# Attention scores as three rounded products of 256 columns instead of one full fp32 product of 192

## The chip, the cores and the metric

The kernel runs on one NeuronCore of a Trainium2 chip, with its engines TensorE (PE, with the weight loads shown apart as PEld), VectorE (DVE), ScalarE (ACT), GpSimd (POOL) and SyncE (SP, which here issues most of the transfers). The metric is the device time of one execution in microseconds; less is better.

## The reference

Local and global attention for 8 batches of 8 heads, followed by a two-layer network on all tokens. Only the parts that the change touches or waits for are kept:

```python
k_all = concat([k_g, k_l]);  v_all = concat([v_g, v_l])          # 32 global + 512 local keys, head_dim 64
out_g = softmax(q_g @ k_all.T / 8) @ v_all                       # 32 global queries see all keys
s_ll  = where(abs(i - j) <= 32, q_l @ k_l.T / 8, -1e9)           # local queries: a band of +-32 ...
s_lg  = q_l @ k_g.T / 8                                          # ... and all global keys
out_l = softmax(concat([s_lg, s_ll])) @ concat([v_g, v_l])
x = heads side by side of concat([out_g, out_l])                 # 4352 tokens x 512
h = x @ w_in;  g = max(h, 0) + log1p(exp(-abs(h)))               # 512 -> 2048
return g @ w_out                                                 # 2048 -> 512
```

## The kernel before

**The network part.** Tokens are handled in eight batches `b` of 512 local tokens, and a ninth of the 256 global ones. In a batch, 16 slices `f` of 128 hidden columns follow each other. `hpart` makes `h` for a slice by 12 matmuls of 512 columns, `act` turns it into `e` (three ACT passes, one DVE pass) and splits it into a high half `gh` (a cast on ACT to fp32r, the rounded 4-byte type that TensorE streams in one pass) and a low half `gl` (a subtraction on POOL). `opart` makes the output from the products `gh*wo_high`, `gh*wo_low` and `gl*wo_high`, 12 matmuls a slice, one or two slices later. The weights are split in the same way (`split_w`: casts on ACT, L498, subtractions on POOL, L499) while batch 0 runs; the last of them is `wo15`.

**The attention part.** Heads are taken in 32 pairs `m`, head 0 on partitions 0 to 63 and head 1 on 64 to 127. Pairs 0 to 5 run ahead of the network in a way of their own. Pairs 6 to 31 are cut in pieces that are dealt out between the matmuls of the network: three score pieces `(m, p)`, p = 0 to 2, then the maxima, probabilities, sums, `values` and `normalise`. A score piece takes one tile `raw` of queries and keys (544 columns for p = 0 and 1, 448 for p = 2), and makes two parts of scores, each for both heads: 128 keys stand still as weights and 192 query columns stream past them (96 in the second part of p = 2). For pairs 8 and later the mask is added on DVE (L325) on the way from the accumulator `s_ps` to `s`, then a transposing maximum goes to `mt` (L326).

**What sets the order.** PE, ACT, DVE, POOL and SP each run their instructions strictly in the order in which they were placed. A scheduler sets the order on each engine by its own estimate of when an operation could start; the PE order follows the text of the kernel. `fold` copies `mt` (or `zt`, the sums) between partition groups on POOL (L339), reduces it on DVE (L342 to L346) and spreads it (L352); then come two transposes `mb` (L360). `normalise` reads the values' accumulator `v_ps` on DVE (L407 to L409). Once the first output accumulators of the network are open, early in batch 0, `s_ps` and `v_ps` share one accumulator tile, `ps_a` tag "a", so the first score piece of the next pair waits until L409 is done.

**Tiles.** `raw` has three buffers. `pl.tile(..., tag="x", bufs=2)` names a place with two buffers; the early pairs used "x" for their exponentials. All matmuls go through the helper `mm`, so they stand under its line (L127) in the profile. One fp32 matmul is shown as two matmul instructions with two weight loads, an fp32r matmul as one of each.

Of the kernel before, what the change touches and what calls it, by code (L numbers as in the profile page):

```python
# [8 lines left out]
F32 = mybir.dt.float32  # L9
F32R = mybir.dt.float32r  # L10
# [3 lines left out]
ALU = mybir.AluOpType  # L14
# [5 lines left out]
P = 128  # L20
# [4 lines left out]
QW = (288, 288, 192)  # L25
KWID = (256, 256, 256)
# [3 lines left out]

M0 = 6
MPE = 8
VAL = 22
TOT = 18
STEP = 3
# [14 lines left out]
def windows(ap2d, start, stride, count, width):  # L50
    base = ap2d[:, start:start + width]
    return bass.AP(base.tensor, base.offset, [list(base.ap[0]), [stride, count], [1, width]])
# [3 lines left out]
def moe_over_global_local_attention(  # L56
# [11 lines left out]
    nc = tc.nc  # L68
    PSUM = bass.MemoryType.PSUM
    const = ctx.enter_context(tc.tile_pool(name="const", bufs=1))  # L70
    pl = ctx.enter_context(tc.tile_pool(name="pl", bufs=2))
# [20 lines left out]
    for o, w, base, sign in ((32, 32, 0, 1), (64, 32, -96, -1), (96, 128, 32, 1), (96, 128, 32, -1)):  # L92
        r = mask0[:, 0, 1, o:o + w]
# [26 lines left out]
    def after(i, what):  # L120

        if what in order:
            tc.add_manual_dep(i.ins, order[what].name, mybir.DependencyInfo(mybir.DependencyClass.NoSync, mybir.DependencyReason.DATA), reason="order")
        return i

    def mm(*a, **k):
        order["pe"] = after(nc.tensor.matmul(*a, **k), "pe").ins  # L127


    M = B * H // 2  # L130
    st = {}
# [153 lines left out]
    def load(m, p):  # L285
        w = QW[p] + KWID[p]
        raw = pl.tile([P, 544], F32, tag="raw", name=f"raw{m}_{p}", bufs=3)
        order["load"] = nc.sync.dma_start(out=raw[:, :w], in_=qk[m - M0, :, EW[p]:EW[p] + w]).ins
        st["raw", m, p] = raw

    def load_v(m):
        t = pl.tile([P, 2, 6, D], F32, tag="v", name=f"v{m}", bufs=2)
        nc.sync.dma_start(out=t.rearrange("p h c d -> p (h c d)"), in_=v[m - M0])
        st["v", m] = t

    def scores(m, p):
        raw = st.pop(("raw", m, p))
        q = QW[p]
        if "o" not in banks:
            ps = ps_s.tile([P, 2, 512], F32, tag=("oA", "oB")[(3 * m + p) % 2], name=f"s_ps{m}_{p}")  # L300
        else:
            ps = ps_a.tile([P, 2, 512], F32, tag="a", name=f"s_ps{m}_{p}")
        parts = ((0, 0, 192), (192, 96, 192 if p < 2 else 96))
        pe_mask = m < MPE
        masks = (mask[:, 0:192], mask[:, 192:384] if p < 2 else mask5)
        for i, (o, qs, w) in enumerate(parts):
            ks = q + 128 * i
            for h in range(2):
                r = slice(64 * h, 64 * h + 64)
                mm(ps[:, h, o:o + w], lhsT=raw[r, ks:ks + P], rhs=raw[r, qs:qs + w],  # L310
                   start=True, stop=not pe_mask, skip_group_check=True)
            for h in range(2 if pe_mask else 0):
                mm(ps[:, h, o:o + w], lhsT=ident, rhs=masks[i], start=False, stop=True, skip_group_check=True)
        if p == 0:
            st["mt", m] = pl.tile([P, 348], F32, tag="mt", name=f"mt{m}", bufs=2)
            nc.gpsimd.memset(windows(st["mt", m], 0, 36, 3, 3), LOW)
        mt = st["mt", m]
        nb = 12 if p < 2 else 9
        s = pl.tile([P, 2, 32 * nb], F32, tag="s" if p < 2 else "s2", name=f"s{m}_{p}", bufs=4 if p < 2 else 2)
        if pe_mask:  # L320
            nc.scalar.copy(s, ps[:, :, 0:32 * nb])  # L321
        else:
            for o, mk in ((0, mask[:, 0:384]),) if p < 2 else ((0, mask[:, 0:192]), (192, mask5)):
                w = mk.shape[1]
                nc.vector.tensor_tensor(s[:, :, o:o + w], ps[:, :, o:o + w], mk.unsqueeze(1).to_broadcast([P, 2, w]), op=ALU.add)  # L325
        order["scores"] = nc.vector.tensor_reduce(windows(mt, 3 + 12 * p, 36, 2, nb), s.rearrange("p h (b k) -> p h b k", k=32),  # L326
                                axis=AX.X, op=ALU.max, apply_transpose=True).ins
        st["s", m, p] = s
# [20 lines left out]
    def maxima(m):  # L349
        e = fold(st.pop(("mt", m)), ALU.max)  # L350
        for a in range(1, 4):
            i = nc.vector.tensor_copy(e[32 * a:32 * a + 32, 0:42], e[0:32, 0:42]).ins  # L352
        order["maxima"] = i
        st["e", m] = e

    def probs(m, p):
        s, e = st["s", m, p], st["e", m]
        k = QW[p] // 32
        mb = pl.tile([P, 2, 288], F32, tag="mb", name=f"mb{m}_{p}", bufs=2)
        nc.vector.transpose(mb[:, :, :QW[p]].rearrange("p h (s k) -> p h s k", k=32),  # L360
                            windows(e, 7 * p, 21, 2, k).unsqueeze(3).to_broadcast([P, 2, k, 32]))
        for h in range(2):
            if p < 2:
                sw = s[:, h].rearrange("p (c w) -> p c w", w=192)
                nc.gpsimd.tensor_tensor(sw, sw, windows(mb[:, h], 0, 96, 2, 192), op=ALU.subtract)  # L365
        if p == 2:
            nc.gpsimd.tensor_tensor(s[:, :, 0:192], s[:, :, 0:192], mb[:, :, 0:192], op=ALU.subtract)
            nc.gpsimd.tensor_tensor(s[:, :, 192:288], s[:, :, 192:288], mb[:, :, 96:192], op=ALU.subtract)
        nc.scalar.activation(s, s, AF.Exp, scale=0.125)  # L369
        if p == 0:  # L370
            st["zt", m] = pl.tile([P, 348], F32, tag="zt", name=f"zt{m}", bufs=2)
            nc.gpsimd.memset(windows(st["zt", m], 0, 36, 3, 3), 0.0)
        nb = 12 if p < 2 else 9
        nc.vector.tensor_reduce(windows(st["zt", m], 3 + 12 * p, 36, 2, nb), s.rearrange("p h (b k) -> p h b k", k=32),  # L374
                                axis=AX.X, op=ALU.add, apply_transpose=True)

    def totals(m):
        e = fold(st.pop(("zt", m)), ALU.add)
        nc.vector.tensor_scalar(e[0:32, 0:42], e[0:32, 0:42], 1e-9, None, op0=ALU.add)
        nc.vector.reciprocal(e[0:32, 0:42], e[0:32, 0:42])  # L380
        for a in (2, 3, 1):
            o = 21 * (a // 2)
            nc.vector.tensor_copy(e[32 * a:32 * a + 32, 0:21], e[0:32, o:o + 21])
        rb = st["rb", m] = pl.tile([P, 640], F32, tag="rb", name=f"rb{m}", bufs=1)
        nc.vector.transpose(rb.rearrange("p (s k) -> p s k", k=32), e[:, 0:20].unsqueeze(2).to_broadcast([P, 20, 32]))

    def values(m):

        vt = st["v", m]
        ps = st["vs", m] = ps_a.tile([P, 2, 512], F32, tag="a", name=f"v_ps{m}")  # L390
        flat = ps.rearrange("p a q -> p (a q)")
        for p in range(NPC):
            s = st.pop(("s", m, p))
            for i, (o, qs, w) in enumerate(((0, 0, 192), (192, 96, 192 if p < 2 else 96))):
                c = OUT[p] + qs
                for h in range(2):
                    mm(flat[64 * h:64 * h + 64, c:c + w], lhsT=vt[:, h, 2 * p + i], rhs=s[:, h, o:o + w],
                       start=p < 2 and i == 0, stop=True, skip_group_check=True)
# [17 lines left out]
    def pieces():  # L416
        def piece(*fs):
            def go():
                for f in fs:
                    f()  # L420
            return go
        ps = []
        for m in range(M0, M):
            for p in range(NPC):
                fs = [lambda m=m, p=p: scores(m, p)]
                if m + 1 < M:
                    fs.append(lambda m=m, p=p: load(m + 1, p))
                if p == 2:
                    fs.append(lambda m=m: maxima(m))
                    fs += [lambda m=m, q=q: probs(m, q) for q in range(NPC)]  # L430
                ps.append((12 * m + 4 * p, piece(*fs)))
            ps.append((12 * m + TOT, lambda m=m: totals(m)))
            fs = [lambda m=m: values(m), lambda m=m: normalise(m)]
            if m + 2 < M:
                fs.append(lambda m=m: load_v(m + 2))
            ps.append((12 * m + VAL, piece(*fs)))
        ps.sort(key=lambda t: t[0])
        return ps
# [173 lines left out]
    def loads(upto):  # L612
        while wk[0] < min(upto, len(order_w)):
            if order_w[wk[0]]:
                load_w(*order_w[wk[0]])
            wk[0] += 1
# [12 lines left out]
    for p in range(NPC):  # L629
        load(M0, p)  # L630
    load_v(M0)
    load_v(M0 + 1)
    loads(W_PRE + 1)
    first = 12 * (H // 2 - 1) + VAL + STEP
    pcs = pieces()
# [5 lines left out]
    n = len(steps)  # L641
# [6 lines left out]
    for k in range(-2, n + 2):  # L648
# [9 lines left out]
        if held:  # L658
            r = bits_w(*held)
# [91 lines left out]
```

## Time and profile before

| | |
|---|---|
| median of 3 runs (lowest to highest) | 1004.74 us (1004.15 to 1005.12) |
| the profiled execution's own time | 1005.01 us |
| its span, first to last instruction | 1003.2 us |
| mean granted TensorE clock | 0.987 |
| score matmul instructions of pairs 6 to 31 | 624, of which 552 belong to pairs 9 to 31 |

The profile is of one execution. Busy time of an engine is the union of its instructions' times; a matmul's shown time is its latency, longer than the spacing at which matmuls follow each other. Rows of the timeline have the start, the time from the first start to the last end of the instructions merged into the row, the engine, the line, the operation, out and in, the shape, the count, and in brackets the idle time ahead of it on its engine and what ended it.

### The profile page before, as it was taken

The page shows a single profiled execution, that of the slowest core. Times are in us where ns is not written, and L with a number is a line of the kernel's source. Part 1 is how long each engine was busy: PE and PEld are TensorE (multiplying, and loading weights), DVE is VectorE, ACT ScalarE, POOL GpSimd, SP SyncE. Part 2 cuts the span into 40 slices and gives each one's busy share as a digit, 9 for nine tenths or more (in the row PEclk, how much of TensorE's full clock was granted, in tenths as well). Part 3 has the DMA queues.
Part 4 walks back from the last instruction along what each step waited for, and adds up shares of the span by engine and source line. Part 5 has one row for each costly group of instructions (what it writes and reads, how often), then busy time and mean ns, then how long its engine had stood idle before and what let it go on. Part 6 is the DMA issues. An engine that isn't in the chain of part 4 may idle for free.

```text
span 1003.2 us, 14264 instructions
## 1 busy us (share of the span) xinstructions
PE 966.0 (96%) x5151; PEld 755.1 (75%) x5151; DVE 645.8 (64%) x1348; ACT 517.5 (52%) x918; POOL 446.1 (44%) x603
## 2 busy tenths in 40 slices
PE   6798989899999999999999999999999999999996
PEld 4576767677777777777777777777777778888895
DVE  6885979856678766776667677776677665211210
ACT  5787656544445544454454444554445445444452
POOL 5664776524444444453345444444435344222221
PEclk9999989989999999999999999999999999999998
DMA  9824322211112111121112111211112100100000
GB/s 354 310 74 144 112 83 60 58 63 48 40 49 90 49 37 48 49 85 43 47 34 90 40 49 49 70 58 49 48 39 89 47 2 16 50 1 1 22 22 21
DMA packets 34302, 66.19 MB, mean 66 GB/s; under 512 B 7608, under 2 KB 11448, under 8 KB 34232
## 3 DMA queue, kind: packets, MB, share of 16 engines
q1 hardware_dynamic: 33416, 65.19, 20.4%
q8 instruction: 40, 0.66, 0.3%
q14 instruction: 30, 0.25, 0.1%
q10 hardware_dynamic: 816, 0.10, 0.1%
HBM read 55.84 MB, written 9.44 MB: 65 GB/s over the span
## 4 chain that ended last, share of the span: by engine, by line
PE 79%; DVE 1%; POOL 0%; issue 0%; ACT 0%; DVEq 0%; POOLq 0%
PE o L127 35%; PE h L127 34%; PE s_ps L127 5%; PE v_ps L127 5%; DVE xl L454 1%; DVE zt L374 0%; POOL wo L499 0%; DVE mb L360 0%; POOL gl L548 0%; DVE wbitswo L490 0%; DVE e L544 0%; ACT ot L566 0%; DVE wlastwo L493 0%; DVE mt L352 0%; DVE mt L342 0%
## 5 line engine op out<-in xcount | busy, mean ns | idle before, releaser
L127 PE MATMUL o<-wo,gh 128*128 128x512 f32 x1088 | 347.5, 400 | 6.2 <-ACT gh L547 4.9
L127 PE MATMUL h<-xh,wi 128*128 128x512 f32 (+1 forms) x1152 | 351.1, 388 | 1.2 <-DVE e L544 0.7
L548 POOL TENSOR_TENSOR gl<-e,gh 128x512 fp32r<-128x512 f32 x136 | 177.8, 1307 | 333.2 <-ACT gh L547 271.1
L127 PEld LDWEIGHTS h<-xh,wi 128*128 128x128 f32 x1152 | 210.3, 190 | 51.4 <-issue 5.6
L127 PEld LDWEIGHTS o<-wo,gh 128*128 128x128 f32 x1088 | 200.9, 189 | 58.3 <-ACT gh L547 5.8
L544 DVE SCALAR_TENSOR_TENSOR e<-h,e 128x512 f32<-128x512 f32 x136 | 93.0, 684 | 234.4 <-ACT e L543 213.9
L127 PE MATMUL h<-xl,wi 128*128 128x512 f32 (+1 forms) x576 | 220.5, 383 | 0.0
L127 PE MATMUL o<-wo,gl 128*128 128x512 f32 x544 | 216.2, 397 | 2.5 <-POOL gl L548 2.5
L541 ACT ACTIVATE e<-h 128x512 f32<-128x512 f32 x136 | 81.3, 598 | 232.2 <-PE h L127 232.2
L547 ACT CAST gh<-e 128x512 fp32r<-128x512 f32 x136 | 84.3, 620 | 112.6 <-DVE e L544 112.6
L365 POOL TENSOR_TENSOR s<-s,mb 128x384 f32<-128x384 f32 x104 | 107.0, 1060 | 51.1 <-DVE mb L360 51.1
L127 PEld LDWEIGHTS h<-xl,wi 128*128 128x128 f32 x576 | 109.0, 189 | 22.7
L127 PEld LDWEIGHTS o<-wo,gl 128*128 128x128 f32 x544 | 102.9, 189 | 27.1 <-POOL gl L548 3.3
L543 ACT ACTIVATE e<-e,one 128x512 f32<-128x512 f32 x136 | 98.4, 723 | 4.2
L542 ACT ACTIVATE e<-e 128x512 f32<-128x512 f32 x136 | 85.7, 630 | 3.4
L325 DVE TENSOR_TENSOR s<-s_ps,mask 128x768 f32<-128x768 f32 (+1 forms) x96 | 64.7, 695 | 29.4 <-PE s_ps L127 29.4
L369 ACT ACTIVATE s<-s 128x768 f32<-128x768 f32 (+1 forms) x78 | 61.7, 790 | 37.1 <-POOL s L365 34.7
L374 DVE TRANSPOSE_TENSOR_REDUCE zt<-s 128x24 f32<-128x768 f32 (+1 forms) x78 | 69.9, 902 | 6.3 <-ACT s L369 4.7
L326 DVE TRANSPOSE_TENSOR_REDUCE mt<-s 128x24 f32<-128x768 f32 (+1 forms) x78 | 69.3, 888 | 5.8 <-ACT s L321 5.1
L127 PEld LDWEIGHTS s_ps<-raw 64*128 64x128 f32 x624 | 48.7, 186 | 29.6 <-issue 22.1
L127 PE MATMUL s_ps<-raw 64*128 64x192 f32 (+1 forms) x624 | 70.1, 340 | 0.7 <-ACT e_g L174 0.7
L127 PEld LDWEIGHTS v_ps<-s,v 128*64 128x64 f32 x624 | 42.5, 137 | 14.3 <-issue 9.0
(134 smaller groups left out, 881.9 us busy)
## 6 DMA issues: line engine op xcount, KB each, us to landing
raw<-in_qk SPq DMA_DIRECT2D x52, 272.0 KB, 2.7
v<-in_v SPq DMA_DIRECT2D x26, 384.0 KB, 3.1
out<-ot SPq DMA_DIRECT2D x34, 256.0 KB, 2.1
wiraw<-in_w_in SPq DMA_DIRECT2D x16, 512.0 KB, 9.1
woraw<-in_w_out SPq DMA_DIRECT2D x16, 512.0 KB, 8.6
raw<-in_qk SPq DMA_DIRECT2D x26, 224.0 KB, 2.5
v<-in_v SPq DMA_DIRECT2D x6, 512.0 KB, 6.0
raw<-in_qk SPq DMA_DIRECT2D x6, 416.0 KB, 7.8
```

What stands on the lines that cost most here:

```text
L127: order["pe"] = after(nc.tensor.matmul(*a, **k), "pe").ins
L325: nc.vector.tensor_tensor(s[:, :, o:o + w], ps[:, :, o:o + w], mk.unsqueeze(1).to_broadcast([P, 2, w]), op=ALU.add)
L326: order["scores"] = nc.vector.tensor_reduce(windows(mt, 3 + 12 * p, 36, 2, nb), s.rearrange("p h (b k) -> p h b k", k=32), axis=AX.X, op=A ...
L365: nc.gpsimd.tensor_tensor(sw, sw, windows(mb[:, h], 0, 96, 2, 192), op=ALU.subtract)
L369: nc.scalar.activation(s, s, AF.Exp, scale=0.125)
L374: nc.vector.tensor_reduce(windows(st["zt", m], 3 + 12 * p, 36, 2, nb), s.rearrange("p h (b k) -> p h b k", k=32), axis=AX.X, op=ALU.add, a ...
L541: nc.scalar.activation(e, ph, AF.Abs)
L542: nc.scalar.activation(e, e, AF.Exp, scale=-1.0)
L543: nc.scalar.activation(e, e, AF.Ln, bias=one)
L544: nc.vector.scalar_tensor_tensor(e, ph, 0.0, e, op0=ALU.max, op1=ALU.add)
L547: nc.scalar.copy(gh, e)
L548: nc.gpsimd.tensor_tensor(gl, e, gh.bitcast(F32), op=ALU.subtract)
```

## The change

For pairs 9 to 31 a new step, `split_qk`, splits a whole `raw` tile (queries and keys together) into a high half, cast to fp32r on ACT, and a low half, subtracted on POOL, both in one tile with two buffers in place "x". It is written behind the scores of the piece ahead of it. The score piece then adds three fp32r products (keys high by queries high, keys high by queries low, keys low by queries high) in place of one fp32 product. Each streams 256 columns; the last 64 of the first part are written over by the second part, and those of the second part are not read. In p = 2 the second part streams 256 columns too, where 96 are used.

```diff
+SPLIT = 9
...
+    def split_qk(m, p):
+
+        raw, w = st.pop(("raw", m, p)), QW[p] + KWID[p]
+        t = st["halves", m, p] = pl.tile([P, 2, 544], F32R, tag="x", name=f"qk{m}_{p}", bufs=2)
+        nc.scalar.copy(t[:, 0, :w], raw[:, :w])
+        nc.gpsimd.tensor_tensor(t[:, 1, :w], raw[:, :w], t[:, 0, :w].bitcast(F32), op=ALU.subtract)
...
+        if m >= SPLIT:
+            t = st.pop(("halves", m, p))
+            products = ((t[:, 0], t[:, 0]), (t[:, 0], t[:, 1]), (t[:, 1], t[:, 0]))
+        else:
+            raw = st.pop(("raw", m, p))
+            products = ((raw, raw),)
         for i, (o, qs, w) in enumerate(parts):
             ks = q + 128 * i
-            for h in range(2):
-                r = slice(64 * h, 64 * h + 64)
-                mm(ps[:, h, o:o + w], lhsT=raw[r, ks:ks + P], rhs=raw[r, qs:qs + w],
-                   start=True, stop=not pe_mask, skip_group_check=True)
+            wide = 256 if m >= SPLIT else w
+            for n, (kt, qt) in enumerate(products):
+                for h in range(2):
+                    r = slice(64 * h, 64 * h + 64)
+                    mm(ps[:, h, o:o + wide], lhsT=kt[r, ks:ks + P], rhs=qt[r, qs:qs + wide],
+                       start=n == 0, stop=n == len(products) - 1 and not pe_mask, skip_group_check=True)
...
                 fs = [lambda m=m, p=p: scores(m, p)]
+                then = (m, p + 1) if p < 2 else (m + 1, 0)
+                if SPLIT <= then[0] < M:
+                    fs.append(lambda then=then: split_qk(*then))
```

PE, the third score piece of pair 19 inside batch 3, before:

```order
L127 MATMUL o3_3_4147<-wo8_1319,gh3_8_4518 128x512 x2
L127 MATMUL o3_3_4147<-wo8_1319,gl3_8_4519 128x512
L127 MATMUL s_ps19_2_4627<-raw19_2_4398 128x192 x2
L127 MATMUL s_ps19_2_4627<-raw19_2_4398 128x96 x2
L127 MATMUL h3_11_4669<-xh3_0_3996,wi10_1230 128x512 x2
L127 MATMUL h3_11_4669<-xl3_0_3997,wi10_1230 128x512
```

The same place after:

```order
L128 MATMUL o3_3_4436<-wo8_1319,gh3_8_4862 128x512 x2
L128 MATMUL o3_3_4436<-wo8_1319,gl3_8_4863 128x512
L128 MATMUL s_ps19_2_4982<-qk19_2_4916 128x256 x12
L128 MATMUL h3_11_5035<-xh3_0_4274,wi10_1230 128x512 x2
L128 MATMUL h3_11_5035<-xl3_0_4275,wi10_1230 128x512
```

Four fp32 matmuls (two of 192 columns, two of 96) have become twelve of 256; their neighbours, and the place of every score piece among the network's matmuls, are the same.

POOL, where batch 0 ends, before (`wo15` is the last weight, `gl0_15` the last low half of batch 0):

```order
L316 MEMSET mt10_2278 128x3x3
L339 COPY zt8_1884<-zt8_1884 32x75 x3
L499 TENSOR_TENSOR wo15_1920<-wlastwo_1918,wo15_1920 128x512
L548 TENSOR_TENSOR gl0_15_1977<-e0_15_1971,gh0_15_1976 128x512
L372 MEMSET zt10_2432 128x3x3
L548 TENSOR_TENSOR gl1_0_2067<-e1_0_2061,gh1_0_2066 128x512
```

The same place after:

```order
L331 MEMSET mt10_2322 128x3x3
L354 COPY zt8_1887<-zt8_1887 32x75 x3
L297 TENSOR_TENSOR qk9_2_2112<-raw9_2_1869,qk9_2_2112 128x448
L517 TENSOR_TENSOR wo15_1923<-wlastwo_1921,wo15_1923 128x512
L566 TENSOR_TENSOR gl0_15_1980<-e0_15_1974,gh0_15_1979 128x512
L387 MEMSET zt10_2501 128x3x3
L297 TENSOR_TENSOR qk10_0_2209<-raw10_0_2022,qk10_0_2209 128x544
```

A subtraction of `split_qk` now stands ahead of `wo15` and `gl0_15`.

POOL, inside batch 3, before (`mt18` are the copies of the maxima of pair 18):

```order
L339 COPY zt17_4178<-zt17_4178 32x75 x3
L548 TENSOR_TENSOR gl3_4_4281<-e3_4_4275,gh3_4_4280 128x512
L372 MEMSET zt19_4654 128x3x3
L548 TENSOR_TENSOR gl3_5_4315<-e3_5_4309,gh3_5_4314 128x512
L548 TENSOR_TENSOR gl3_6_4374<-e3_6_4368,gh3_6_4373 128x512
L339 COPY mt18_4262<-mt18_4262 32x75 x3
L365 TENSOR_TENSOR s18_0_4264<-s18_0_4264,mb18_0_4411 128x384 x2
```

The same place after:

```order
L566 TENSOR_TENSOR gl3_4_4592<-e3_4_4586,gh3_4_4591 128x512
L354 COPY zt17_4478<-zt17_4478 32x75 x3
L297 TENSOR_TENSOR qk19_0_4728<-raw19_0_4578,qk19_0_4728 128x544
L566 TENSOR_TENSOR gl3_5_4626<-e3_5_4620,gh3_5_4625 128x512
L387 MEMSET zt19_5020 128x3x3
L566 TENSOR_TENSOR gl3_6_4696<-e3_6_4690,gh3_6_4695 128x512
L297 TENSOR_TENSOR qk19_1_4846<-raw19_1_4648,qk19_1_4846 128x544
L354 COPY mt18_4570<-mt18_4570 32x75 x3
L380 TENSOR_TENSOR s18_0_4572<-s18_0_4572,mb18_0_4744 128x384 x2
```

Each pair's copies of the maxima now stand behind a subtraction of the next pair's queries and keys.

More of the change, by code (lines that the diff above doesn't have):

```diff
@@ L296, in scores @@
     def scores(m, p):
-        raw = st.pop(("raw", m, p))
         q = QW[p]
```

## The prediction, made before the run

> **What bounds the kernel now.** I read the page first: busy times, the slices, the chain of work that ended last.
>
> ```profile
> PE 966.0 (96%) x5151; PEld 755.1 (75%) x5151; DVE 645.8 (64%) x1348; ACT 517.5 (52%) x918; POOL 446.1 (44%) x603
> PE   6798989899999999999999999999999999999996
> PE 79%; DVE 1%; POOL 0%; issue 0%; ACT 0%; DVEq 0%; POOLq 0%
> L127 PE MATMUL s_ps<-raw 64*128 64x192 f32 (+1 forms) x624 | 70.1, 340 | 0.7 <-ACT e_g L174 0.7
> ```
>
> From the ninth slice of 25 us on PE is full, and the chain is PE almost alone. So a nanosecond added to PE there is a nanosecond of time, and work on ACT and POOL costs nothing as long as PE doesn't come to wait for it. The scores' 0.7 us of waiting says that no load of `raw` holds them up. Next the table by stretches (span, busy time and count of PE, PEld, DVE, ACT, POOL, granted clock, DMA share, GB/s): the end of batch 0, and one whole later batch.
>
> ```profile
> 165.00:205.00 40.00, 35.62 (x172) 27.09 (x171) 34.64 (x66) 21.55 (x38) 23.75 (x25) 0.96 0.17 50
> 421.50:531.00 109.50, 109.50 (x578) 84.95 (x580) 79.25 (x175) 53.55 (x86) 49.76 (x73) 1.00 0.19 54
> ```
>
> In the later batch PE is busy for all 109.50 us at full clock. At the end of batch 0 it idles 4.4 us, and DVE is nearly full there. The change starts with pair 9, whose pieces lie in that stretch and behind it.
>
> **What a score piece costs PE today.** The timeline of PE around a piece of p = 0 or 1 (first three rows), one of p = 2 (next two), and narrow cuts into the first piece that show its pairs of matmuls and weight loads:
>
> ```profile
> 640.00 0.39 PE L127 MATMUL o<-wo,gl 128*128 128x512 f32 x1
> 640.32 0.92 PE L127 MATMUL s_ps<-raw 64*128 64x192 f32 x8
> 641.17 0.73 PE L127 MATMUL o<-wo,gh 128*128 128x512 f32 x2
> 657.61 0.79 PE L127 MATMUL s_ps<-raw 64*128 64x192 f32 x8
> 658.33 0.73 PE L127 MATMUL h<-xh,wi 128*128 128x512 f32 x2
> ...
> 640.32 0.30 PEld L127 LDWEIGHTS s_ps<-raw 64*128 64x128 f32 x4 [0.36 <-issue]
> 640.58 0.65 PE L127 MATMUL s_ps<-raw 64*128 64x192 f32 x6
> 640.59 0.36 PEld L127 LDWEIGHTS s_ps<-raw 64*128 64x128 f32 x4
> 640.75 0.19 PEld L127 LDWEIGHTS s_ps<-raw 64*128 64x128 f32 x2
> 640.91 0.33 PE L127 MATMUL s_ps<-raw 64*128 64x192 f32 x2
> ```
>
> From the first score matmul to the next large one it takes 0.85 us (p = 0, 1) or 0.72 us (p = 2). The two heads use different halves of the rows, and their matmuls run as a pair: six matmuls from 640.58 on, the last two together at 640.91, make two pair spacings in 0.65 - 0.33 = 0.325 us, so 0.163 us a pair, 0.65 us for four. The other 0.20 us is the first load, not hidden, and the emptying of the array before the next matmul. The loads of the next pair begin at 640.59, as the pair at 640.58 begins, and are hidden.
>
> **What it costs afterwards.** No row shows fp32r matmuls of 64 rows, so their pair spacing is bounded. The nearest rows are the network's fp32r matmuls of 256 columns and 128 rows, each with its own weight load, at the end of the program: 24 in a row, first and last shown.
>
> ```profile
> 947.86 0.28 PE L127 MATMUL h<-xh,wi 128*128 128x256 f32 x1
> 950.54 0.28 PE L127 MATMUL h<-xl,wi 128*128 128x256 f32 x1
> 29.88 0.50 PE L127 MATMUL s0g<-raw,raw 128*128 128x32 f32 x3
> 30.10 0.28 PE L127 MATMUL s0g<-raw,raw 128*128 128x32 f32 x1
> ```
>
> They follow each other every (950.54 - 947.86)/23 = 0.1165 us. From below the spacing is bounded by the weight load: in the last two rows three matmuls of only 32 columns start between 29.88 and 30.10, so 0.11 us apart. From above, two heads that don't overlap would take 2 x 0.1165 = 0.233 us. I take 0.1165, since the fp32 pairs of the same shape overlap fully; and 0.11 to 0.122 as its range.
>
> Six pairs are then 0.70 us in place of four (0.65 us): p = 0 and 1 cost 0.05 us more, so 0.90 us. In p = 2 the sum is the same 0.90 us, against 0.72: 0.18 us more, since fp32 saved there with 96 columns what 256 now throws away. With 23 pairs (9 to 31): 46 x 0.05 + 23 x 0.18 = 2.3 + 4.1 = 6.4 us on PE. With 0.11: 46 x 0.01 + 23 x 0.14 = 3.7 us; with 0.122: 46 x 0.08 + 23 x 0.21 = 8.5 us.
>
> **The splits.** The nearest rows are the network's own cast and subtraction of 512 columns and a subtraction of 384, by shape:
>
> ```profile
> L547 ACT CAST gh<-e 128x512 fp32r<-128x512 f32 x136 | 84.3, 620 | 112.6 <-DVE e L544 112.6
> L548 POOL TENSOR_TENSOR gl<-e,gh 128x512 fp32r<-128x512 f32 x136 | 177.8, 1307 | 333.2 <-ACT gh L547 271.1
> L365 POOL TENSOR_TENSOR s<-s,mb 128x384 f32<-128x384 f32 x104 | 107.0, 1060 | 51.1 <-DVE mb L360 51.1
> ```
>
> By columns the cast of 544 takes 0.65 us and that of 448 0.56; the subtractions 1.37 and 1.18 us (two ns a column between 384 and 512). In all 46 x 0.65 + 23 x 0.56 = 43 us more on ACT and 46 x 1.37 + 23 x 1.18 = 90 us more on POOL. Per pair that is 1.9 us of ACT and 3.9 us of POOL in 27 us, where they now work 13 us each: there is room. What counts is who is queued behind them.
>
> - *The low halves of `g`.* A cast waits for the buffer that the score piece two splits back frees, and the activations behind it on ACT wait too. I looked for the tightest place in the batches that hold splits, the first slice of a batch:
>
> ```profile
> 650.87 1.29 POOL L548 TENSOR_TENSOR gl<-e,gh 128x512 fp32r<-128x512 f32 x1 [2.44 <-issue]
> 655.24 0.40 PE L127 MATMUL o<-wo,gl 128*128 128x512 f32 x1
> ```
>
> PE takes this `gl` 3.1 us after it is ready. A cast (0.65 us), up to 0.9 us of waiting for the piece ahead, or a subtraction (1.37 us) fit in. Cost zero; if all three added up, 2.9 us, the cover is just used.
>
> - *The copies of the maxima*, which now stand behind a subtraction (third place in the order above). Behind them on DVE lies `normalise`, and for its L409 the next pair's first score piece waits, since they share an accumulator:
>
> ```profile
> 549.49 1.30 POOL L548 TENSOR_TENSOR gl<-e,gh 128x512 fp32r<-128x512 f32 x1 [1.44 <-ACT gh L547]
> 550.85 0.80 POOL L339 COPY mt<-mt 32x75 f32<-32x75 f32 x3
> 555.73 0.51 DVE L409 TENSOR_TENSOR xa<-v_ps,rb 128x352 f32<-128x352 f32 x1
> 558.14 0.43 PE L127 MATMUL s_ps<-raw 64*128 64x192 f32 x2
> ```
>
> L409 ends at 556.24, 1.9 us before PE needs the tile. Here POOL is busy right up to the copies, so the whole 1.37 us is passed on, and 0.5 us is left. Cost zero, with a thin cover; it is a rival below.
>
> - *The last weight*, second place in the order: POOL, then PE, then PE's clock (the 0.50 of the last row) in the stretch behind.
>
> ```profile
> 198.53 1.18 POOL L339 COPY zt<-zt 32x75 f32<-32x75 f32 x3 [3.04 <-DVE zt L374]
> 199.82 1.29 POOL L499 TENSOR_TENSOR wo<-wlastwo,wo 128x512 fp32r<-128x512 f32 x1
> 201.06 1.28 POOL L548 TENSOR_TENSOR gl<-e,gh 128x512 fp32r<-128x512 f32 x1
> 200.34 0.50 PE L127 MATMUL o<-wo,gh 128*128 128x512 f32 x1 [3.33 <-ACT gh L547]
> 201.17 0.50 PE L127 MATMUL o<-wo,gh 128*128 128x512 f32 x1 [0.32 <-POOL wo L499]
> 202.40 0.80 PE L127 MATMUL o<-wo,gl 128*128 128x512 f32 x1 [0.73 <-POOL gl L548]
> 202.40:208.20 5.80, 5.80 (x14) 0.50 0.24 90
> ```
>
> PE already waits here for both subtractions, so the 448-column one ahead of them goes straight to the time: 1.2 us. The clock falls to 0.50 after the idle time. If a longer idle time keeps it there half as long again, 2.9 us more, of which half is lost: 1.5 us. Not below zero: nothing is taken off that path. I take 1.2, range 0 to 3.
>
> *Transfers.* Their number and sizes stay; a `raw` load now waits for the subtraction that read its buffer, earlier than the score piece did. The load of `wo15`'s raw data on SP's queue comes to stand behind one of pair 10 that waits for pair 8's second piece, which is long done by then; no cost.
>
> **The sum.** 6.4 + 1.2 = 7.6 us on the profiled execution's 1005.01 us, so 1012.6; that execution lies 0.27 us above the median, so I say 1012.3 us, 0.76% slower. With the bounds of both terms: 3.7 to 11.5 us more, 1008.4 to 1016.2.
>
> **A rule on weight loads.** The row: the loads at 640.59 run beside matmuls in the same two halves of the rows. The Trainium skill says otherwise ("TensorE: Matmul & The Clock Gate", Part 3: Packing small matmuls): a weight load overlaps matmuls in flight only where the row group differs. By the row the sum is 1012.3 us, by the rule 1050 us, the third rival's time. For fp32 the trace doesn't agree with the rule; for fp32r of 64 rows no run so far shows it.
>
> **The rivals.**
> 1. *PE comes to wait for L409.* For: 0.5 us of cover, and a subtraction on POOL takes longer where other engines work beside it, as the weights' did (1603 ns for 512 columns, where `gl` takes 1307):
>
> ```profile
> L499 POOL TENSOR_TENSOR wo<-woraw,wo 128x512 fp32r<-128x512 f32 x15 | 24.0, 1603 | 8.4 <-ACT wo L498 8.0 <-POOL zt L339 0.5
> ```
>
> Against: it is the tightest of four such places in a batch; elsewhere POOL idles before the copies. It decides once POOL delays the copies by over 1.9 us. At 0.3 to 0.5 us a pair, 7 to 11 us on top: about 1021 us. 12%.
> 2. *Pairs of fp32r matmuls don't overlap.* Twice the rate of results of the fp32 pairs is something that no row shows. Then six pairs cost 0.70 us more a piece: 69 x 0.70 = 48 us, 1060 us. 6%.
> 3. *The weight loads of the new pairs are not hidden.* Then five of a piece's six loads stand open. One takes 0.11 us until the next may begin (two rounds from 640.32 on take 0.30 us, the last one by itself 0.19): 69 x 5 x 0.11 = 38 us, 1050 us. Against: the fp32 loads, and those of the 24 matmuls of 256 columns, are hidden. 3%.
> 4. *It gets faster, since the array no longer empties.* Each piece loses about 0.1 us to emptying and 0.1 us to an open load, on entry and on exit. If a change of number type causes this, it goes, as the neighbours are fp32r: 69 x 0.4 = 28 us less, 1005.0 + 7.6 - 28 = 985 us. Against it stands a place with fp32 on both sides:
>
> ```profile
> 51.62 0.55 PE L127 MATMUL s<-raw 64*128 64x224 f32 x4
> 51.81 0.36 PE L127 MATMUL s<-raw 64*128 64x224 f32 x2
> 52.09 0.32 PE L127 MATMUL o0g<-p0g0gh,v 128*128 128x64 f32 x1
> ```
>
> Pairs follow each other every 0.19 us, but the matmul of 128 rows comes after 0.28: 0.09 us are lost without any change of type. 5%.
> 5. *Nearly nothing is added.* The pairs stream as fast by the column as fp32 does in its two passes, 0.163 x 256/384 = 0.109 us, six in 0.65, and the last weight's wait is covered: p = 0 and 1 cost nothing, p = 2 0.13 us, 23 x 0.13 = 3.0 us, 1007.7 us. 8%.
>
> **How the numbers follow.** The forecast has 66%, the rivals 12, 6, 3, 5 and 8%. The predicted time is the forecast's, 1012.3 us. From 1006.5 to 1023 us lie the forecast, the first rival and most of the fifth, some 84%. A measurement of this kernel tells about 0.2% (2 us) from no change: faster 5% (the fourth rival), same 4% (the lower half of the fifth), slower 91%.
>
> **What would show it.** In the profile after, 828 score matmuls of 64x256; the pair spacing in a narrow cut, 0.11 to 0.12; from first score matmul to next large one 0.90 us in all three pieces; PE full with no idle time in the later batches; the waits before `wo15` longer by 1.2 us. I am wrong if idle time of PE ahead of `s_ps` appears, released by DVE; if pairs come 0.2 us or more apart; or if the 0.20 us around a piece shrinks.

## The result, and the profile after

| | before | after |
|---|---|---|
| median (lowest to highest) | 1004.44 us (1003.79 to 1005.12) | 1017.4 us (1016.42 to 1018.38) |
| the profiled execution, its span | 1005.01 us, 1003.2 us | 1017.3 us, 1015.3 us |

The changed kernel takes 1.0129 times as long (95% interval 1.0111 to 1.0147), 13.0 us more by the medians and 12.1 us by the two spans. Forecast were 7.6 us more, 1012.3 us. Lines are now those of the changed kernel: L361 is the spread copy of the folds (L346 before), L394 the addition of 1e-9 (L379), L398 the copies behind it (L383), L562 is `e`, L566 `gl`, L517 the subtraction of a weight, L296 and L297 the new cast and subtraction.

The page, the score products' group, and the two stretches that were shown of before:

```profile
PE 974.8 (96%) x5427; PEld 764.0 (75%) x5427; DVE 663.0 (65%) x1348; ACT 553.4 (55%) x987; POOL 535.4 (53%) x672
PE 77%; DVE 2%; POOL 1%; issue 1%; ACT 0%; POOLq 0%; DVEq 0%
L128 PE MATMUL s_ps<-qk 64*128 64x256 f32 x828 | 67.5, 295 | 0.0
165.00:208.00 43.00, 35.57 (x174) 26.43 (x173) 37.87 (x68) 22.52 (x39) 26.55 (x28) 0.95 0.20 61
424.00:534.50 110.50, 110.36 (x624) 86.12 (x623) 81.37 (x172) 59.81 (x98) 65.22 (x84) 1.00 0.19 54
```

DVE has as many instructions as before (1348) and is busy 17 us longer, although nothing was added to it. On the chain of work that ended last PE has lost two points, and DVE, POOL and issue have gained one each. In the later batch 0.14 us show as idle on PE, where before there was none. No wait stands at the 828 score matmuls, and a narrow cut into a piece of p = 0 has the forecast's spacing:

```profile
657.48 0.97 PE L128 MATMUL s_ps<-qk 64*128 64x256 f32 x12
658.38 0.50 PE L128 MATMUL h<-xh,wi 128*128 128x512 f32 x1
...
657.70 0.75 PE L128 MATMUL s_ps<-qk 64*128 64x256 f32 x10
657.82 0.63 PE L128 MATMUL s_ps<-qk 64*128 64x256 f32 x8
```

Cuts that leave off one pair more each begin 0.12 us apart; over all pieces the spacing is 0.118 us. Over the 13 pieces between 300 and 420 us the mean from the first score matmul to the next large one is 0.907 us, against 0.851 (p = 0 and 1) and 0.720 us (p = 2) before: 46 x 0.056 + 23 x 0.187 = 6.9 us. The other 5 us are waits. The table of PE's waits, the two rows of before first:

```profile
PE h L127 <- DVE e L544: 0.7, 2, 0.4
PE o L127 <- POOL wo L499: 0.3, 1, 0.3
PE h L128 <- DVE e L562: 2.2, 3, 1.2
PE o L128 <- POOL wo L517: 1.4, 1, 1.4
```

The wait for the last weight grew by 1.1 us; the one for DVE's `e` by 1.5 us and more (behind each such wait a weight load stands open, and short ones don't show). Here is one place of five alike, slice 2 of batch 5: above the dots the spread copy and `e` before, below them DVE, POOL and PE after.

```profile
649.33 0.16 DVE L346 COPY zt<-zt 32x6 f32<-32x6 f32 x1
649.40 0.67 DVE L544 SCALAR_TENSOR_TENSOR e<-h,e 128x512 f32<-128x512 f32 x1
...
659.64 1.04 DVE L361 COPY zt<-zt 32x6 f32<-32x6 f32 x1
660.72 0.17 DVE L394 TENSOR_SCALAR zt<-zt 32x42 f32<-32x42 f32 x1
660.82 0.67 DVE L562 SCALAR_TENSOR_TENSOR e<-h,e 128x512 f32<-128x512 f32 x1
659.27 1.39 POOL L297 TENSOR_TENSOR qk<-raw,qk 128x544 fp32r<-128x544 f32 x1 [0.53 <-POOL zt L354]
660.33 0.39 PE L128 MATMUL h<-xl,wi 128*128 128x512 f32 x1
660.56 0.62 PE L128 MATMUL h<-xh,wi 128*128 128x512 f32 x2
661.02 0.39 PE L128 MATMUL h<-xl,wi 128*128 128x512 f32 x1
661.54 0.72 PE L128 MATMUL h<-xh,wi 128*128 128x512 f32 x2
```

A copy of 32 x 6 elements takes 1.04 us and ends at 660.68, just after POOL's subtraction (660.66). `e` stands behind it on DVE, and now behind L394 too, which came after `e` before (L379). The next `h` needs the accumulator that `e` reads; it starts 0.52 us after the matmul ahead of it, where 0.23 is usual (660.33 to 660.56). Since a matmul's shown time is its latency (0.39 us), little of this is idle time by the profile, and the table of waits leaves it out; the starts tell it.

A second hold-up lies 16 us ahead of this one, and adds to it. DVE subtracts two tiles in SBUF there (L472, the low half of `x`) while POOL makes another of the new subtractions; below the dots the same DVE instruction in run 3 of the experiments, which has no such subtraction:

```profile
641.39 1.37 POOL L297 TENSOR_TENSOR qk<-raw,qk 128x544 fp32r<-128x544 f32 x1
641.81 1.10 DVE L472 TENSOR_TENSOR xl<-xa,xh 128x128 fp32r<-128x128 f32 x1
...
637.53 0.25 DVE L472 TENSOR_TENSOR xl<-xa,xh 128x128 fp32r<-128x128 f32 x1
```

From there to the sums DVE has no idle time that could make good the 0.85 us. So the fold of the sums starts 0.9 us later against the score piece than in run 3, and the 0.88 us of L361 come on top.

In batch 0 the same happens twice, with the weights' bit shift (L506) held up as well:

```profile
163.90 1.59 DVE L506 TENSOR_SCALAR wbitswo<-wbitswo 128x512 int32<-128x512 int32 x1
165.42 1.27 DVE L361 COPY zt<-zt 32x6 f32<-32x6 f32 x1
166.61 0.67 DVE L562 SCALAR_TENSOR_TENSOR e<-h,e 128x512 f32<-128x512 f32 x1
162.90 2.31 POOL L297 TENSOR_TENSOR qk<-raw,qk 128x544 fp32r<-128x544 f32 x1
165.18 1.50 POOL L517 TENSOR_TENSOR wo<-woraw,wo 128x512 fp32r<-128x512 f32 x1
170.07 2.70 DVE L398 COPY zt<-zt 32x21 f32<-32x21 f32 x3
167.34 0.72 PE L128 MATMUL h<-xh,wi 128*128 128x512 f32 x2 [0.59 <-DVE e L562]
175.47 0.72 PE L128 MATMUL h<-xh,wi 128*128 128x512 f32 x2 [1.24 <-DVE e L562]
```

L506 ends at 165.49 (POOL's subtraction at 165.21), L361 at 166.69 (the weight's at 166.68). Ahead of the second wait three copies take 2.70 us, where three took 0.54 us in slice 2 of batch 5 before (L383 at 652.80). Following the starts of the `gl` matmuls through both traces gives where the span grew: 2.3 us by slice 12 of batch 0 (these two waits, with a weight load left open behind each), 0.7 us at the batch's end (the last weight, after what its longer wait gives back), then 1.63 us in each of five batches, of which 1.2 are score pieces and 0.4 the wait in slice 2 (batch 1 has the pieces alone). In sum 6.9 + 2.3 + 0.7 + 5 x 0.4 = 11.9 of 12.1 us.

### The profile page after: what moved, and what is told of

Same layout as the page of the kernel before. It is cut to its first block, busy times and chain, and to the rows that moved or that the text cites. A ratio compares the mean times of both kernels' runs of the same rounds, so it can differ in the third digit from the quotient of the medians.

```text
span 1015.3 us, 15015 instructions
## 1 busy us (share of the span) xinstructions
PE 974.8 (96%) x5427; PEld 764.0 (75%) x5427; DVE 663.0 (65%) x1348; ACT 553.4 (55%) x987; POOL 535.4 (53%) x672
## 4 chain that ended last, share of the span: by engine, by line
PE 77%; DVE 2%; POOL 1%; issue 1%; ACT 0%; POOLq 0%; DVEq 0%
PE o L128 34%; PE h L128 32%; PE s_ps L128 6%; PE v_ps L128 5%; DVE zt L361 1%; DVE xl L472 0%; DVE e L562 0%; DVE zt L357 0%; POOL zt L354 0%; POOL s L382 0%; DVE mb L375 0%; POOL gl L566 0%; POOL wo L517 0%; POOL qk L297 0%; DVE zt L394 0%
## 5 line engine op out<-in xcount | busy, mean ns | idle before, releaser
L566 POOL TENSOR_TENSOR gl<-e,gh 128x512 fp32r<-128x512 f32 x136 | 177.5, 1305 | 292.3 <-ACT gh L565 281.4
L562 DVE SCALAR_TENSOR_TENSOR e<-h,e 128x512 f32<-128x512 f32 x136 | 92.1, 678 | 190.8 <-ACT e L561 172.9
L297 POOL TENSOR_TENSOR qk<-raw,qk 128x544 fp32r<-128x544 f32 (+1 forms) x69 | 91.3, 1323 | 23.8 <-ACT qk L296 20.1
L128 PEld LDWEIGHTS s_ps<-qk 64*128 64x128 f32 x828 | 53.3, 185 | 25.0 <-issue 21.4
L128 PE MATMUL s_ps<-qk 64*128 64x256 f32 x828 | 67.5, 295 | 0.0
```

Of the source, the lines that this page charges most:

```text
L297: nc.gpsimd.tensor_tensor(t[:, 1, :w], raw[:, :w], t[:, 0, :w].bitcast(F32), op=ALU.subtract)
L562: nc.vector.scalar_tensor_tensor(e, ph, 0.0, e, op0=ALU.max, op1=ALU.add)
L566: nc.gpsimd.tensor_tensor(gl, e, gh.bitcast(F32), op=ALU.subtract)
```

## The experiments

**1 and 2: the two halves of the change by themselves.** Their edits (first the splits alone, then the products alone):

```diff
-        raw, w = st.pop(("raw", m, p)), QW[p] + KWID[p]
+        raw, w = st["raw", m, p], QW[p] + KWID[p]
...
-            t = st.pop(("halves", m, p))
-            products = ((t[:, 0], t[:, 0]), (t[:, 0], t[:, 1]), (t[:, 1], t[:, 0]))
+        raw = st.pop(("raw", m, p))
+        products = ((raw, raw),)
...
-            wide = 256 if m >= SPLIT else w
+            wide = w
```
```diff
-            t = st.pop(("halves", m, p))
+            t = st["halves", SPLIT, 0]
-                if SPLIT <= then[0] < M:
+                if then == (SPLIT, 0):
```

> The halves are made for pairs 9 to 31 as in the changed kernel, but no product reads them: the scores are the fp32 product of raw, as before. So the 6.9 us that the narrow cuts give for the products (46 x 0.056 + 23 x 0.187) go, and what is left of the 13 us is the price of the splits. Three theories on the other 5 to 6 us: A, POOL's two-input subtractions hold up DVE's copies while both run, so the network's e comes late to PE; B, ACT's casts wait for a score piece to free their buffer, and the activations behind them come late; C, the subtractions only stand ahead of the last weight, of gl and of the copies in POOL's queue. Here nobody reads the halves, so a cast never waits for PE, and B has only the last weight left. A: 5 to 6 us over before, about 1010, with the waits of 0.3 us ahead of h in slice 2 of the batches still there. B: 1 us over, about 1005.5, those waits gone. C: 5 to 6 us over, like A. My forecast, which took the splits at 1.2 us: 1005.6.

> The other half of the change alone: one tile of raw is split once, and all 69 later score pieces make their three fp32r products from it (the other pieces' splits are left out, so the scores aren't those of the reference). All three theories: only the products' own time is added, 46 x 0.056 + 23 x 0.187 = 6.9 us, so 1011.3, with no wait ahead of h in slice 2 and the short wait ahead of wo15 of the kernel before. If the score pieces themselves cost more than the cuts show (a wait elsewhere that they cause), it stays above 1013; if the sum with the split alone exceeds 13 us by more than 1 us, the two halves share a cost.

Measured: 1017.77 us (ratio 1.0133, 1.0119 to 1.0146) and 1026.12 us (1.0210, 1.0196 to 1.0224). Neither fits any theory, and both for a reason of their own. The waits of the first on ACT and PE, then one of the second between 215 and 250 us, and some of its transfers between 200 and 250 us:

```profile
ACT qk L296 <- DMA raw<-in_qk: 83.7, 46, 2.6
PE o L128 <- POOL gl L566: 6.9, 6, 1.8
...
DVE ot L586 <- DMA out<-ot: 8.3, 1, 8.3
raw<-in_qk SPq DMA_DIRECT2D x29, 272.0 KB, 3.3
```

In the first, `raw` is held until the score piece again, so its next load comes late and 46 casts wait for transfers, 83.7 us in all, with `gh` queued behind them on ACT. In the changed kernel the subtraction gives `raw` back early, and no cast waits for a load. In the second nobody reads the later `raw` tiles, so their loads aren't held back by a reader: 43 of them (29 of 272 KB, 14 of 224 KB) run between 200 and 250 us, DVE waits 8.3 us for an output store there, and one stretch loses 13 us (the starts of the `gl` matmuls are 14.65 us late after it, 1.65 before it). Leaving out a reader changed when transfers start. Behind that stretch the second run loses 6.5 us more, about the products' own time, and slice 2 has no wait. What the splits cost neither run tells.

**3: without the low half.**

```diff
-        nc.gpsimd.tensor_tensor(t[:, 1, :w], raw[:, :w], t[:, 0, :w].bitcast(F32), op=ALU.subtract)
-            products = ((t[:, 0], t[:, 0]), (t[:, 0], t[:, 1]), (t[:, 1], t[:, 0]))
+            products = ((t[:, 0], t[:, 0]),) * 3
```

> As the changed kernel, but without the low half: no subtraction on POOL, the high half is used in all three products. The casts on ACT and their wait for the score piece stay. A: the waits ahead of h in batch 0 and in the five later batches go, DVE's spread copies (L361) take 0.16 us again where they took 1.0 to 1.3, and the wait ahead of wo15 is back at 0.3 us: 1004.4 + 6.9 = 1011.3 us. B: the waits ahead of h stay (2.3 us in batch 0, 2.0 us later), only the last weight's 0.7 us go: 1016.5 us. C: as A in time, but the copies' times would not have mattered.

Measured: 1011.44 us (1.0070, 1.0057 to 1.0082), 6.8 us over before: the products' own 6.9. ACT still casts 69 tiles, and the waits in the later batches are gone, so B falls. L361 on the sums is back at its length:

```profile
L361 DVE COPY zt<-zt 32x6 f32<-32x6 f32 x26 | 4.3, 167 | 0.8
```

**4: a copy on POOL in place of the subtraction.**

```diff
-        nc.gpsimd.tensor_tensor(t[:, 1, :w], raw[:, :w], t[:, 0, :w].bitcast(F32), op=ALU.subtract)
+        nc.gpsimd.tensor_copy(t[:, 1, :w], t[:, 0, :w])
```

> As the changed kernel, but POOL's subtraction of two tiles is replaced by a copy of one (the high half into the place of the low half), in the same place in the code and waiting for the same cast; the low half is left out. This parts A from C. A: a one-input operation on POOL doesn't hold DVE the way a two-input one does, so DVE's copies beside it stay short, the waits ahead of h go, and the time is 1011.5 to 1013 us (something is left for the last weight). C, a matter of POOL's queue alone: if the copy takes as long as the subtraction (1.1 us or more), the waits stay and the time is 1016 to 1017.5 us. If DVE's copies are stretched beside the one-input copies too, any overlap of the two engines holds DVE, whatever the number of inputs.

Measured: 1012.89 us (1.0083, 1.0070 to 1.0097). The time is A's, but not for A's reason. POOL and DVE in slice 2 of batch 5:

```profile
655.34 0.64 POOL L297 CAST qk<-qk 128x544 fp32r<-128x544 f32 x1 [0.85 <-ACT qk L296]
655.41 0.59 DVE L361 COPY zt<-zt 32x6 f32<-32x6 f32 x1
```

L361 is held up beside an operation of one input too, until that ends; it is only shorter (0.64 against 1.39 us), and `e` is in time. So the number of POOL's inputs doesn't matter to this copy, the length of the operation does. The run doesn't part A from C, since the copy is short.

**5: the splits alone, with the buffers freed as in the changed kernel.**

```diff
-            products = ((t[:, 0], t[:, 0]), (t[:, 0], t[:, 1]), (t[:, 1], t[:, 0]))
+            products = ((t[:, 0].bitcast(F32), t[:, 0].bitcast(F32)),)
-            wide = 256 if m >= SPLIT else w
+            wide = w
```

> The splits alone, a second time, with the buffers held and freed by the score piece as in the changed kernel: casts and subtractions are made, and the scores are the one fp32 product of before (192 and 96 columns), from the high half read as fp32; the low half is left out of the scores. The third run gave the three products with the casts 6.8 us over before, so the subtractions are what the rest hangs on. The changed kernel's 13 us less 6.8: 6 us over before, 1010.6 us, with the waits ahead of h in slice 2 and the long wait ahead of wo15 as in the changed kernel. If the subtractions hurt only together with the longer score pieces, 1005 to 1006 us.

Measured: 1010.49 us (1.0061, 1.0047 to 1.0075), 5.6 us over before. With the third run's 6.8 that makes 12.4 of the 13 us: the two halves add up. The waits for `e` are there with short score pieces too: 2.0 us in four waits, the longest 1.2.

**6 and 9: the held operations behind the fold taken away, POOL's subtractions left.** First the copies alone (L398 is shown, L361 and L367 likewise), then the addition too:

```diff
-            nc.vector.tensor_copy(e[32 * a:32 * a + 32, 0:21], e[0:32, o:o + 21])
+            nc.vector.tensor_reduce(e[32 * a:32 * a + 32, 0:21], e[0:32, o:o + 21].unsqueeze(2), axis=AX.X, op=ALU.max)
```
```diff
-        nc.vector.tensor_scalar(e[0:32, 0:42], e[0:32, 0:42], 1e-9, None, op0=ALU.add)
-        nc.vector.reciprocal(e[0:32, 0:42], e[0:32, 0:42])
+        u = e[0:32, 0:42].rearrange("p (h c) -> p h c", h=2)[:, :, 0:20]
+        nc.vector.reciprocal(u, u)
```

> As the changed kernel, nothing left out, but DVE's three copies of the folds (L361, L367, L398) are written as reductions over one element, with the same values. In the traces so far DVE's reductions and transposes take their usual time beside POOL's subtractions, while the copies stand still until POOL's operation is done (L361: 0.16 us alone, 1.04 us beside the subtraction of queries and keys). A, DVE's copies are held up and e behind them is late: the 0.4 us in slice 2 of the five later batches go, and part of the 2.3 us in batch 0, where a shift of the weights' bits (L506) is held up too and stays: 1013 to 1015.4 us. C, the subtractions merely stand ahead of the copies and of gl in POOL's queue: that queue is the same here, so the waits stay and the time is 1017 us.

> In the sixth run the hold-up moved by one instruction: L361, now a reduction, took 0.15 us, but L394 behind it, an addition of 1e-9 on one input, took 0.89 us beside the same subtraction, and e behind it gained only 0.2 us. Here L394 is left out as well (the 1e-9 isn't added), and the reciprocal L395 takes the 20 columns a head that are used. No operation of the kind that was held up then stands between the fold and e. A, DVE held up: no wait is left ahead of h in slice 2 of the later batches, 5 x 0.39 = 2 us less than the changed kernel there, and batch 0 keeps its 3 us or part of them: 1013.5 to 1015.4 us. C, POOL's queue: that queue is as it was, 0.2 us or more of wait stays in each batch, 1016.5 us or above.

Measured: 1016.73 us (1.0116, 1.0102 to 1.0130) for the sixth run: neither theory's number, within 0.4 us of C's. Its starts say otherwise: the growth in batch 0 ahead of the last weight falls from 2.3 to 0.2 us, and the later waits from 0.4 to 0.2 us each. The scheduler made another order of it, though. The trace is 1.8 us behind that of before already before its first split (PE's waits at 133 and 137 us are 1.3 us longer than in the changed kernel), and `gl0_15` stands ahead of `wo15` on POOL, so PE waits 2.6 us for `wo15`, where it was 1.4. The same place in the sixth run, and below the dots in the ninth:

```profile
658.86 1.38 POOL L297 TENSOR_TENSOR qk<-raw,qk 128x544 fp32r<-128x544 f32 x1 [0.57 <-POOL zt L354]
659.20 0.15 DVE L361 TENSOR_REDUCE zt<-zt 32x6 f32<-32x6 f32 x1
659.39 0.89 DVE L394 TENSOR_SCALAR zt<-zt 32x42 f32<-32x42 f32 x1
660.20 0.67 DVE L562 SCALAR_TENSOR_TENSOR e<-h,e 128x512 f32<-128x512 f32 x1
...
654.76 1.38 POOL L297 TENSOR_TENSOR qk<-raw,qk 128x544 fp32r<-128x544 f32 x1 [0.57 <-POOL zt L354]
655.10 0.15 DVE L361 TENSOR_REDUCE zt<-zt 32x6 f32<-32x6 f32 x1
655.28 0.39 DVE L395 RECIPROCAL zt<-zt 32x40 f32<-32x40 f32 x1
655.60 0.62 DVE L562 SCALAR_TENSOR_TENSOR e<-h,e 128x512 f32<-128x512 f32 x1
```

As a reduction L361 takes 0.15 us beside the same subtraction, and the next instruction, one that can be held, is held in its place until 660.28. `e` starts 1.34 us after the subtraction's start; in the changed kernel it was 1.55, in the ninth run 0.84 us. There nothing is held between the fold and `e`, the wait in slice 2 is gone in every later batch, the growth of 2.3 us in batch 0 is gone too, and the time is 1012.00 us (1.0068, 1.0056 to 1.0081), 5.4 us under the changed kernel and below what either theory said. The hold-up of L472 is still there (1.03 us), and alone it costs PE nothing in slice 2. POOL's order isn't the same to the last instruction: some `gl` moved ahead of other operations, at the end of batch 0 ahead of `wo15`. But as many of the new subtractions stand ahead of each of the 136 `gl` as in the changed kernel, in both runs: for the waits for `e` C falls, A stands.

This is what the Trainium skill states ("SBUF — State Buffer", section "Who interferes with whom"): DVE and GpSimd share one pair of ports by an exclusive lock, which DVE's copies, casts and operations with a scalar may take, and which reductions on this chip never need. The rows agree: 1.04 and 0.89 us for the copy and the scalar operation, 0.15 us for the reduction.

**12: the same edit without the change.** L346, L352, L383 and L379 of the kernel before, edited as in the ninth run.

> The ninth run's edit to DVE's copies and its addition, made to the kernel before, without the change: L346, L352 and L383 as reductions over one element, L379 (the 1e-9) left out. It tells whether that edit gains something of its own. In the trace of before L379 takes 857 ns on average, so it is held up beside POOL's operations there too, but PE waits for e only 0.7 us in all. A: the holding up costs the kernel before nearly nothing, since e stands ahead of the held operations or has time: 1003.9 to 1005 us, and the ninth run's gain of 5.4 us belongs to the splits. If the edit gains by itself, 2 us or more below before (1002.9 or less), that much of the ninth run's gain isn't the splits'.

Measured: 1003.38 us (0.9984, 0.9975 to 0.9993), 1.6 us under the kernel before and between the two forecasts. By the starts nearly all of it is won in batch 0, before the place of the first split. Each against its own runs of before, the changed kernel takes 13.0 us more and the ninth run 7.1, so 5.9 us were won there. If 1.6 of them are the edit's own there too, 4.3 us are the splits', the amount that the starts gave (2.3 + 5 x 0.4). The kernel before had the hold-up too, mostly where it costs nothing:

```profile
L379 DVE TENSOR_SCALAR zt<-zt 32x42 f32<-32x42 f32 x26 | 22.3, 857 | 0.7
```

The same instruction takes 0.17 us where nothing holds it up, as L394 at 660.72 above; and yet PE waits for `e` only 0.7 us in all of that kernel.

**7: the low half on DVE.** `nc.gpsimd.tensor_tensor` becomes `nc.vector.tensor_tensor`.

> As the changed kernel, nothing left out, but the low half is subtracted on DVE instead of POOL. POOL's queue is then that of before, so what the subtractions did to DVE's copies, to gl and to wo15 goes; DVE gets 69 subtractions of 0.5 to 0.6 us, or up to 1.3 us where one runs beside an operation of POOL (as L472 does): 40 to 60 us more on DVE, which works 81 of 110 us in a batch. A and C: if they fit between e and the others, 1011.4 to 1013 us. If DVE becomes late for e or for normalise by them, 1015 us or more, with waits of PE released by DVE.

Measured: 1026.89 us (1.0224, 1.0210 to 1.0237). The subtractions' group and PE's waits for DVE:

```profile
L297 DVE TENSOR_TENSOR qk<-raw,qk 128x544 fp32r<-128x544 f32 (+1 forms) x69 | 74.7, 1083 | 10.3 <-ACT qk L296 9.7
PE h L128 <- DVE e L562: 6.6, 8, 1.1
PE s_ps L128 <- DVE xa L424: 5.3, 7, 1.0
```

74.7 us come to DVE, at 1083 ns each, beyond the 40 to 60 us expected. They are held up themselves: 23 of those of 544 columns, at whose start POOL idles or is nearly done, take 0.7 us, the other 23 take 1.4 us, and those of 448 columns 1.2 us. Now both `e` and `normalise` are late: the forecast's first rival, which the change itself didn't wake, shows here.

**8: 192 columns.** `wide = 256 if m >= SPLIT else w` becomes `wide = w`.

> As the changed kernel, nothing left out, but the three products stream 192 columns, and 96 in the second part of p = 2, where the changed kernel streams 256. If fp32r streams a column as fast at 192 columns as at 256, the pairs are bounded by their weight loads at 0.11 us: six take 0.66 in place of 0.71 us, 69 x 0.04 = 3 us less, 1014.5 us. If below 256 columns it falls to the rate of one fp32 pass (0.163 us for 192 columns): p = 0 and 1 cost 6 x 0.163 = 0.98 us, 0.27 more, p = 2 some 0.1 more, 46 x 0.27 + 23 x 0.1 = 15 us more, 1032 us. If it falls to a quarter of its rate (four times 0.46 ns a column: 0.35 us for 192): 1.4 us more a piece, 1.1 in p = 2, 90 us more, 1107 us.

Measured: 1011.18 us (1.0065, 1.0052 to 1.0077), 6.2 us under the changed kernel. Cuts into a piece, then slice 2 of batch 5:

```profile
653.40 0.72 PE L128 MATMUL s_ps<-qk 64*128 64x192 f32 x10
653.51 0.61 PE L128 MATMUL s_ps<-qk 64*128 64x192 f32 x8
...
654.94 1.39 POOL L297 TENSOR_TENSOR qk<-raw,qk 128x544 fp32r<-128x544 f32 x1 [0.94 <-POOL zt L354]
654.99 0.67 DVE L562 SCALAR_TENSOR_TENSOR e<-h,e 128x512 f32<-128x512 f32 x1
655.59 0.78 DVE L394 TENSOR_SCALAR zt<-zt 32x42 f32<-32x42 f32 x1
```

A pair takes 0.11 us, the spacing that the prediction read for weight loads, and no longer than one of 256 columns (0.118): neither of the slower rates of the forecast shows, and the 64 spare columns bought nothing. Pieces fall to 0.844 us (p = 0 and 1) and 0.80 us (p = 2), 46 x 0.063 + 23 x 0.107 = 5.4 us. More comes from an accident of order: with shorter pieces the scheduler put `e` ahead of L394 on DVE, so the held operation (0.78 us) has nothing urgent behind it, and slice 2 has no wait, 5 x 0.4 = 2.0 us. That is A a second time, with every instruction still there. The two make 7.4 us; the 6.2 are less, since the trace is 0.9 us behind that of the changed kernel already before the first split, for which no cause was isolated.

**10 and 11: later pairs.** `SPLIT = 9` becomes 12; then 192 columns as well.

> As the changed kernel, but from pair 12 on instead of 9, so that no split lies in batch 0. Products: 40 x 0.056 + 20 x 0.187 = 6.0 us. The five later waits of 0.39 us stay: 2.0 us. If the rest (2.3 us of waits for e and some 0.7 us for the last weight) is due to the splits meeting the crowded end of batch 0, it goes: 1004.6 + 8.0 = 1012.6 us. If it is a price of starting to split anywhere, it comes back in the batch where pair 12 starts: 1015.5 us.

> Both edits that helped: products of 192 columns (96 in the second part of p = 2), and pairs 12 to 31 alone. By the narrow cuts of the eighth run a piece takes 0.844 us for p = 0 and 1 (0.851 with fp32) and 0.80 for p = 2 (0.72): 20 x 0.08 - 40 x 0.007 = 1.3 us. That run had no wait in the later batches, since there e stands ahead of L394 in DVE's order: 1006 us if it is so here, 1008 us if the waits of slice 2 come back. It would be the cheapest form of the change; faster than before it isn't by any of the theories.

Measured: 1013.10 us (1.0077, 1.0065 to 1.0090), and 1007.03 us (1.0020, 1.0011 to 1.0029). PE's waits in the tenth run are those of before: 0.5 us for `e` (0.7 before), 0.3 us for the last weight.

The five later waits are still there by the starts, as expected (0.5 us more in the two slices around slice 2 of a batch, where 0.1 is left without the wait). The 3 us in batch 0 belong to its crowded end and not to the start of splitting. The eleventh run has no wait in slice 2. It is the cheapest form of the change here and still 2.1 us slower than before: for a pair of heads three products take 2 x 0.844 + 0.80 = 2.49 us of PE, fp32 2 x 0.851 + 0.72 = 2.42 us.

## Why the prediction was right or wrong

The direction was right, and 1017.4 us lie in the stated range of 1006.5 to 1023, but the second by luck. The sum with the bounds of both its terms ends at 1016.2 us. The range reaches further for the first rival, PE waiting for L409, and that didn't come; another wait filled its place.

- *Six pairs at the pace of the network's fp32r matmuls of 256 columns, 6.4 us.* Right: 6.9 us by the cuts, 6.8 us by the third run. 0.118 us a pair was taken as 0.1165. The second rival (no overlap) and the third (open weight loads) are out, and with the third the rule on weight loads: the Trainium skill's "TensorE: Matmul & The Clock Gate", Part 3: Packing small matmuls, would have given 38 us more. The fifth (3.0 us) is out by the 6.9 us, the fourth since a piece is 0.20 us longer than its six pairs, as before (0.907 - 6 x 0.118). How much of the 0.20 us is the open load and how much the emptying, no run shows.
- *The last weight, 1.2 us.* Right as a wait (0.3 to 1.4 us); some 0.4 us of it was won back behind it.
- *Cost zero for `gl`, the copies of the maxima and L409, transfers.* Right: PE's wait for `gl` didn't grow, and no wait for L409 shows.
- *"What counts is who is queued behind them."* This is the step that failed. The splits were priced by ACT's and POOL's queues alone; what a POOL operation does to the instruction that runs on DVE at that moment was not asked. The sum has no term for it, and it is 4.3 us of the 12.1: DVE's copies, L506 and L472 wait for POOL's subtractions, `e` behind them comes late, and PE waits for `e`. The cover of `gl` (3.1 us) was taken as that of the batch's tightest place, but the network waits by a second way: `h` needs the accumulator that `e` on DVE gives back.
- *"PE full with no idle time in the later batches."* Wrong, by 0.4 us in each of five batches. The row that could have told was in the trace of before: L379 at 857 ns for 32 x 42 elements, where L383's copies of 32 x 21 take 222. The prediction did quote POOL's weights at 1603 ns beside `gl`'s 1307, but read it as POOL being slowed, in a rival for L409.

The price of the last weight's longer wait and its return is from the starts of matmuls in one pair of traces; no run isolated it.

## What to carry to other kernels

Before work is put on an engine with room, look in the trace for small operations of other engines that take far longer than their size asks: a 32 x 6 copy of 1 us that ends with its neighbour's operation is a hold-up, and what stands behind it sets the price. It can be moved off by another form of the same operation or by placing the urgent instruction ahead. An experiment that leaves out a reader also changes when buffers come free: cut so that tiles are still held and freed by the same instructions.

## What was not expected of the hardware

- DVE's copies and scalar operations in SBUF stand still until the operation that runs on POOL ends: L361 0.16 us alone, 0.59 us beside a 0.64 us copy, 1.04 us beside a 1.39 us subtraction. A subtraction of two tiles in SBUF stands still too (L472 0.25 us alone, 1.10 us beside a 1.37 us subtraction). Reductions (0.15 us), the reciprocal (0.39) and `e`, which reads an accumulator (0.67), aren't touched.
- fp32r pairs of 64 rows run at 0.118 us with 256 columns and 0.11 us with 192; fp32 takes 0.163 us a pass with 192.
